# Turning one batch's x on TensorE instead of by transposing transfers, in a fused attention and highway layer

## The chip, the core and the metric

The kernel runs on one core of one Trainium2 chip. The time is that of one execution in device microseconds (us), from the first to the last thing the core does; lower is better. A profile is one execution recorded instruction by instruction. Engines are called as the profile calls them: PE is the matmul engine (PEld its weight loads, which overlap), DVE the vector engine, ACT the scalar engine, POOL the general one, SP the one that here only issues transfers. "DVEq" or "SPq" is an engine's queue of issued work. SBUF is the on-chip memory that transfers and all engines reach, PSUM the small memory that PE writes its products to, in banks.

## What is computed

Attention with cosine scores over 8 batches of 12 heads, 448 tokens of 64 numbers each, then a gated layer over the 3584 tokens with all 12 heads side by side (768 numbers a token). Cut to what matters:

```python
q_n = q / (norm(q) + 1e-6);  k_n = k / (norm(k) + 1e-6)
attn = softmax(q_n @ k_n.T / tau) @ v            # (8, 12, 448, 64)
x = attn.transpose(0, 2, 1, 3).reshape(3584, 768)
H = maximum(x @ w_h, 0)
T = 1 / (1 + exp(-(x @ w_t + b_t)))
out = T * H + (1 - T) * x                        # float32
```

The kernel works in 16-bit floats between the two ends.

## The kernel before

**Work units.** A batch has six head pairs; they are numbered through, pair s = 6 * batch + p, from 0 to 47. Tokens of a batch are three blocks of 128 and a tail of 64. For a pair, q and k rows are scaled to length one (`scaled`, ops named qn and kn; on POOL or DVE), turned so that the 64 head numbers lie across partitions (`turn`: for batches 0 to 3 seven transposes on PE and a copy cpT out of PSUM; for batches 4 to 7, the tuple `BY_DMA`, one transposing transfer for two pairs on SP's queue, line 570, and one for the tails, line 597), multiplied (`scores`: three ops qk and one qkt on PE, each followed by an exponential on ACT, lines 646 and 662), and multiplied with v (`attend`: three ops av and a tail avt on PE; then a reciprocal rc, line 720, and the scaled output ev, line 722, on DVE, which writes the pair's columns of the tile x). Squares, their sums in halving steps (fa, fb, fc) and the inverse root (nt, or ln and re on ACT for batches 0 to 2) come a batch ahead (`square`, `newton`).

**The gated layer.** When the six pairs of a batch have written x, `ffn` (line 742 on) runs it in four groups, i = 0 to 3: three of 128 tokens and the tail of 64; groups are numbered g = 4 * batch + i. A group needs its x turned, with the 768 numbers across partitions; the turned x lies in the tile xT, a half of a batch in each of its two buffers. There are two ways to turn it. For batches 1 to 6, SP issues two transposing transfers a batch (`xd12` for groups 0 and 1, `xd9` for groups 2 and 3, line 759). For batches 0 and 7, each group has an op xt6 (xt3 for the tail) on PE, that turns six (three) blocks of 128 x 128 against a unit matrix into a pB bank of PSUM (line 765), and a copy cpx6 (cpx3) on DVE from there to xT (line 770). Then PE multiplies with both weights (ops fft3 and fft4 of lines 843 and 850, ffc of the tail at 834), ACT makes the tanh of the gate (874), DVE forms hm (888), gt (893) and gg (896), POOL or DVE adds x (out, 901), and a transfer stores it (910).

**Modes of PE.** Every PE op carries a mode letter: F for products over all 128 partitions (turns, qkt, av, xt), T for two halves of 64 partitions side by side (qk, fft), C for two halves of the output (ffc).

**Buffers.** PSUM has three double banks pS, for scores qk and the products of the gated layer, and two banks pB, for turned blocks, the qkt products and the outputs U of a pair. An op that takes a bank waits until the last reader of its former content is done.

**What sets the order.** The function first makes a list of 1683 ops, each with an engine and what it reads, writes and uses. A written-out permutation, ORDER, says in which order they are issued; each engine works through its own ops in that order, and semaphores carry the waits between engines. SLOTS gives the buffer for each new use of a tile, one digit each, in the same order. MOVED is a set of op numbers: where an op may run on either of two engines, `pick` takes the other one for the numbers in it. URGENT is a set of POOL ops for which the next DVE op of those that share a port with POOL waits. Op numbers count the ops in the order in which the function makes them, so they shift behind an added op.

Of the kernel before, what the change touches and what calls it, by code (L numbers as in the profile page):

```python
# [102 lines left out]
URGENT = frozenset(  # L103
    int(n)
    for n in """
116 117 135 136 154 155 174 192 307 327 345 365 383 403 434 448 502 510 529 548 586 604 636 716 735 754 811 857
916 923 958 976 992 1010 1054 1079 1113 1120 1137 1155 1173 1208 1237 1251 1276 1316 1317 1334 1351 1369 1370
1404 1434 1448 1473 1548 1584
""".split()
# [912 lines left out]
```

## Time and profile before

| what | value |
|---|---|
| three timed runs | 267.65, 266.72, 264.89 us; median 266.72 |
| the profiled execution's own time | 266.79 us |
| its span (first to last instruction) | 265.0 us |
| PE busy | 241.9 us, 91% of the span |
| DVE, ACT, POOL busy | 219.5, 205.5, 120.2 us |
| mean granted clock of PE | 0.995 of full |
| transposing transfers on SP | 12 into xT, 12 into qT, 4 into tT |
| 128 x 128 transposes of x on PE | 42 |

How to read the rows below. A row of the timeline has start, length, engine, line, operation, tiles out and in, shape and count, and in brackets the idle time of the engine before it with what ended that idle. A row of the groups has line, engine, operation, tiles, shapes and count, then busy time in us and the mean of one in ns, then idle before. A row of the stretches has the stretch and its length, then for each engine its busy time and its number of instructions, then PE's granted clock, the mean busy share of the 16 DMA engines (it can pass 1 because packets of several queues overlap) and GB/s. A row of the waits has who waited for whom, total us, number and longest. A length on PE is a pipelined one: the next instruction can start before it ends, so what an op costs PE is read from start to start.

### The profile page before, as it was taken

What the parts mean: (1) busy time and instruction counts of PE and PEld (TensorE: products, weight loads), DVE (VectorE), ACT (ScalarE), POOL (GpSimd) and SP (SyncE); (2) the same over time, 40 slices, a digit from 0 to 9 for tenths busy, and PEclk for the clock granted to TensorE, in tenths of its full rate; (3) what the DMA queues carried; (4) which work ended last, traced back from release to release, by engine and by line L of the source; (5) the groups of instructions that cost most, each with busy time, mean ns of one, the idle gap of its engine ahead of it and who ended that gap; (6) DMA issues with size and microseconds to landing.
All of it is one profiled execution on the core that took longest, in us unless ns stands there. A gap on an engine that the chain in (4) does not pass through costs nothing. (4 is left out here: it accounts for less than half of the span.)

```text
span 265.0 us, 9021 instructions
## 1 busy us (share of the span) xinstructions
PE 241.9 (91%) x3747; PEld 163.4 (62%) x3747; DVE 219.5 (83%) x478; ACT 205.5 (78%) x334; POOL 120.2 (45%) x154
## 2 busy tenths in 40 slices
PE   0787889999999999999999799999999999999990
PEld 0344567667676676667665566567667677667560
DVE  4799999989799999999999969988867774457484
ACT  2279999899988999899989798689877997572130
POOL 8873676384752546714633507244455300123220
PEclk9999999999999999999999999999999999999998
DMA  6999999999999799999899989996665988300244
GB/s 132 199 192 180 178 205 204 194 185 186 165 190 208 116 188 165 175 170 230 174 136 131 153 201 239 154 223 168 144 116 141 218 113 177 118 2 25 112 143 158
DMA packets 103353, 43.12 MB, mean 163 GB/s; under 512 B 97168, under 2 KB 100240, under 8 KB 103312
## 3 DMA queue, kind: packets, MB, share of 16 engines
q0 software_dynamic: 38464, 16.32, 51.3%
q1 hardware_dynamic: 62560, 23.63, 47.8%
q10 hardware_dynamic: 2288, 2.59, 3.4%
q8 instruction: 29, 0.48, 0.7%
q14 instruction: 12, 0.10, 0.1%
HBM read 37.82 MB, written 11.01 MB: 184 GB/s over the span
## 5 line engine op out<-in xcount | busy, mean ns | idle before, releaser
L646 ACT ACTIVATE E<-pS 128x896 f16<-128x896 f32 x144 | 127.7, 931 | 21.5 <-PE pS L640 19.0
L850 PEld LDWEIGHTS <-xT 64*128 64x128 f16 x1152 | 53.5, 94 | 33.8 <-DMA xT<-x 1.7
L850 PE MATMUL pS<-wt,xT 64*128 64x384 f16 x576 | 57.7, 323 | 1.2 <-DMA xT<-x 1.2
L850 PE MATMUL pS<-wh,xT 64*128 64x384 f16 x576 | 56.9, 323 | 0.2 <-DVE hm L888 0.2
L901 POOL TENSOR_TENSOR os<-x,hm 128x768 f32<-128x768 f16 (+1 forms) x15 | 20.9, 1398 | 61.4 <-DVE hm L896 33.7
L640 PE MATMUL pS<-qT 64*128 64x384 f16 x288 | 44.1, 326 | 1.9 <-ACT E L646 1.2
L696 PE MATMUL pB<-vp,E 128*128 128x65 f16 x864 | 44.2, 194 | 0.4 <-ACT E L646 0.4
L696 PEld LDWEIGHTS <-E 128*128 128x128 f16 x864 | 38.7, 98 | 3.0 <-issue 1.0
L888 DVE SCALAR_TENSOR_TENSOR hm<-pS,x 128x768 f16<-128x768 f32 (+1 forms) x32 | 26.8, 839 | 13.4 <-PE pS L850 11.0
L640 PEld LDWEIGHTS <-qT 64*128 64x128 f16 x576 | 23.3, 94 | 17.7 <-issue 4.5
L692 PE MATMUL pB<-vp,Et 128*128 128x130 f16 x144 | 31.9, 222 | 0.8 <-DVE x L722 0.8
L874 ACT ACTIVATE tt<-pS 128x768 f16<-128x768 f32 x24 | 19.5, 821 | 14.9 <-PE pS L850 14.6
L722 DVE SCALAR_TENSOR_TENSOR x<-pB,rd 128x448 f16<-128x448 f32 x48 | 29.6, 619 | 1.1
L662 ACT ACTIVATE Et<-pB 128x64 f16<-128x64 f32 x96 | 29.2, 370 | 1.0 <-PE pB L655 0.8
L640 PE MATMUL pS<-tT,qT 64*128 64x64 f16 x282 | 27.5, 189 | 0.0
L255 POOL TENSOR_TENSOR qn<-kr,rs 128x384 f16<-128x384 f16 x20 | 17.6, 882 | 14.4 <-DVE qn L255 5.4
L720 DVE RECIPROCAL rd<-pB 128x7 f32<-128x7 f32 x48 | 9.6, 199 | 12.8 <-PE pB L696 6.5
L712 PE MATMUL pB<-vp,E 128*128 128x65 f16 x288 | 18.4, 194 | 0.0
L255 POOL TENSOR_TENSOR qn<-qr,rs 128x384 f16<-128x384 f16 x18 | 15.0, 840 | 6.4 <-DVE qn L255 2.8
L307 PE MATMUL pB<-fill 128*128 128x384 f16 x40 | 9.8, 404 | 8.4 <-DVE fill L278 8.4
L896 DVE TENSOR_TENSOR hm<-tt,hm 128x768 f16<-128x768 f16 (+1 forms) x31 | 17.2, 558 | 0.2
L255 POOL TENSOR_TENSOR kb<-kt,rs 64x384 f16<-64x384 f32 x10 | 8.2, 821 | 20.2 <-DVE tt L893 6.9
(117 smaller groups left out, 439.3 us busy)
## 6 DMA issues: line engine op xcount, KB each, us to landing
out_dram<-os SPq DMA_DIRECT2D x20, 384.0 KB, 3.5
vr<-in_v_dram POOLq DMA_DIRECT2D x8, 576.0 KB, 8.6
kr<-in_k_dram POOLq DMA_DIRECT2D x7, 576.0 KB, 14.3
qr<-in_q_dram POOLq DMA_DIRECT2D x7, 576.0 KB, 12.3
qt<-in_q_dram SPq DMA_DIRECT2D x16, 96.0 KB, 6.7
vt<-in_v_dram SPq DMA_DIRECT2D x16, 96.0 KB, 6.7
out_dram<-os ACTq DMA_DIRECT2D x4, 384.0 KB, 3.0
kt<-in_k_dram SPq DMA_DIRECT2D x14, 96.0 KB, 6.4
```

Source lines behind the costliest of these rows:

```text
L255: return (nc.vector if eng == "DVE" else nc.gpsimd).tensor_mul(out_, a, c)
L640: ins = nc.tensor.matmul(dst, lhsT=qT[ln, 384 + 128 * c : 512 + 128 * c], rhs=rhs, start=True, stop=True)
L646: return nc.scalar.activation(R("E", s)[:, c, :, 0:448], R("S", 3 * s + c)[:, :, 0:448], AF.Exp, scale=inv_tau)
L662: ins = nc.scalar.activation(R("Et", s)[:, at : at + n], R("B", ("S", s))[:, lo : lo + n], AF.Exp, scale=inv_tau)
L692: nc.tensor.matmul(U[:, 2 * c : 2 * c + 2, :].rearrange("p g e -> p (g e)"), lhsT=Et[:, 192 + 128 * c : 320 + 128 * c], rhs=vp[:, 6:8, :]. ...
L696: ins = nc.tensor.matmul(U[:, 2 * c + ab, :], lhsT=EF[:, j, 576 * ab + 128 * c : 576 * ab + 128 * c + 128], rhs=vp[:, 3 * ab + j, :], star ...
L712: ins = nc.tensor.matmul(U[:, 6, :], lhsT=lt, rhs=rh, start=(n == 0), stop=(n == 7))
L722: op("DVE", f"ev {s}", lambda: nc.vector.scalar_tensor_tensor(out=R("x", b)[:, :, D * p : D * p + D], in0=U_()[:, :, 0:D], scalar=0.0, in1 ...
L850: ins = nc.tensor.matmul(P[:, h, 0:MH], lhsT=lt, rhs=rh, start=(part == 0 and cc == (-1 if wi == 0 else 0)), stop=(part == 1 and cc == CC ...
L874: return nc.scalar.activation(T.rearrange("p (h m) -> p h m", h=2), P[:, :, 0:MH], AF.Tanh, scale=0.5)
L888: return nc.vector.scalar_tensor_tensor(out=o_, in0=i0, scalar=0.0, in1=xs, op0=ALU.max, op1=ALU.subtract)
L901: op(en, f"out{wd} {g}", lambda: eng.tensor_add(R("os", g)[:, 0:W], xall(), R("hm", g)[:, 0:W]), at + 0.1, r=[("gg", g), ("x", b)], w=[("o ...
```

## The change

x of batch 3, the fourth, is turned the second way: the new tuple `X_ON_PE = (3,)` sends it to the branch of batches 0 and 7. Its two transposing transfers (xd12 and xd9, groups 12 to 15) go; four ops on PE come (xt6 for groups 12, 13, 14 and xt3 for group 15) and four copies on DVE (cpx6, cpx6, cpx6, cpx3). The list has 1689 ops instead of 1683.

ORDER, SLOTS, MOVED and URGENT are all new, so the order on every engine, the buffer of most uses, and the engine of many ops that may run on either are different. The numbers of buffers are the same as before. Counted over the two lists: PE has 669 ops instead of 665, DVE 473 instead of 467, ACT 294 instead of 300, POOL 148 instead of 145, SP 105 instead of 106. By kind, DVE gets four copies of xT, three copies cpT (from ACT), six of v (from ACT and POOL), two of v's tails, one tail output add and three clears; it loses four folds fa and fb of 12 columns and one of 36, three kn, one qn, two norms of query tails and two squares. ACT loses three copies cpT and four of v and gets two squares.

The diff, with the four tables cut to their ends:

```diff
 ORDER = tuple(
     int(n)
     for n in """
-25 23 4 0 20 19 33 5 18 17 21 29 22 16 27 6 24 35 10 26 1 277 28 36 41 11 8 42 7 3 12 73 15 31 87 30 80 43 44 32
...
-1663 1673 1671 1664 1672 1674 1665 1676 1666 1675 1677 1679 1678 1680 1681 1682
+25 23 5 0 20 19 33 16 18 17 21 26 22 7 9 28 4 24 36 10 27 1 12 481 29 35 41 686 32 42 2 3 11 84 6 31 8 80 30 82
...
+1687 1688
...
 URGENT = frozenset(
...
-1404 1434 1448 1473 1548 1584
...
+1357 1358 1375 1411 1454 1520 1572 1607 1638 1671
...
 MOVED = frozenset(
...
-1512 1513 1532 1548 1549 1551 1566 1568 1583 1584 1586 1601 1603 1632 1665
...
+1573 1574 1589 1590 1607 1638 1671
...
     BY_DMA = (4, 5, 6, 7)
     LOGS = 2
+    X_ON_PE = (3,)
     assert (B, NH, S, D) == (8, 12, 448, 64)
...
-        if 1 <= b < B - 1:
+        if 1 <= b < B - 1 and b not in X_ON_PE:
             if not i % 2:
                 hf = i // 2
                 nd = 12 - 3 * hf
```

On PE's new list the four turns stand thus, with their neighbours: fft3 10 1 1, **xt6 12**, qkt 24, fft3 10 0 2; then fft3 12 0 3, **xt6 13**, **xt6 14**, fft3 12 1 3; then qk 26 0, **xt3 15**, av 24 0. (In these names the first number of fft3 is the group, that of qk, qkt and av the head pair.)

More of the change, by code (lines that the diff above doesn't have):

```diff
@@ L91 @@
     for n in """
-0000010100000001000000100011002011000200001101111011001120011211010200021101000210000101210001121100001200010110
-1212120110011101101000010211001002021010102111101212101020011002001020102001021001001001211001021212020010011210
-0001100101001011010200102200010200010102102102212011020000000100212211211000211021120111101000011120011122010002
-0012101102103001020001102011021011002001110021110110221000001020101100200002103101100100021110020011222012100021
-0121011010021210011110112302001121112100002101012010221111201120011010002101220122100012221100220101201100020100
-2011000110310221021211000020010021001001001210020100010220112101111002210320101021121201100201112211101000000210
-0003212210120112000102122111010222201021010110011100100020100012110012201200002111020101320210002122211020022021
-00031201100010110120100020102011212022011001110
+0000011010000100010002001001101001100010000112100010012110121020201000010012010102120001010100120101110001020112
+0011200011110000010200010111022000101102111002101100100200210101210200111002100101012100101121012200211000010000
+2201011102100100200122101001001122001021002022010220122010001102000201120110021010211112011001111021120011010100
+2012003102000102120120110201101200211101112101000100210001010102100120010200230110111200110102100101020022112202
+2101111012010101011101010200203110011001021002102100010120221001100110102110100010121120212110200212101111121000
+1000210111100012011002220022102121110322011002120021010000000020021101212002101120012000011231102010011110203201
+1002001100120121020002211012101100020001021010020012202120110103200111020022200100102012001111121220311111221011
+000012001010201010002111110020120021012020021120301
 """.replace("\n", "")
@@ L105 @@
     for n in """
-116 117 135 136 154 155 174 192 307 327 345 365 383 403 434 448 502 510 529 548 586 604 636 716 735 754 811 857
-916 923 958 976 992 1010 1054 1079 1113 1120 1137 1155 1173 1208 1237 1251 1276 1316 1317 1334 1351 1369 1370
-1404 1434 1448 1473 1548 1584
[3 rows of a table added]
 """.split()
```

143 rows, old and new, of tables (MOVED, ORDER, URGENT) are left out of this document.

## The prediction

> **What bounds the kernel now.** I read the page's engine totals first, then the same totals by stretches, then who PE waited for in the stretch that the change touches, and last the single rows there.
>
> ```profile
> span 265.0 us, 9021 instructions
> PE 241.9 (91%) x3747; PEld 163.4 (62%) x3747; DVE 219.5 (83%) x478; ACT 205.5 (78%) x334; POOL 120.2 (45%) x154
> ```
>
> ```profile
> core 0: us, PE busy (x) PEld busy (x) DVE busy (x) ACT busy (x) POOL busy (x), PEclk, DMA share, GB/s
> 8.00:60.00 52.00, 46.86 (x646) 30.50 (x646) 48.82 (x107) 44.70 (x78) 33.94 (x48) 1.00 1.42 192
> 60.00:110.00 50.00, 49.30 (x812) 34.53 (x811) 47.39 (x102) 45.19 (x73) 27.94 (x34) 1.00 1.26 174
> 110.00:130.00 20.00, 19.97 (x323) 13.42 (x321) 18.80 (x46) 19.22 (x29) 7.44 (x10) 1.00 1.07 192
> 130.00:150.00 20.00, 17.99 (x261) 11.88 (x258) 19.73 (x39) 16.35 (x29) 10.65 (x12) 1.00 1.54 138
> 150.00:170.00 20.00, 19.06 (x336) 12.93 (x332) 16.57 (x37) 17.75 (x30) 6.73 (x7) 1.00 1.12 200
> 170.00:250.00 80.00, 80.00 (x1275) 54.81 (x1273) 54.48 (x117) 58.03 (x94) 23.70 (x28) 1.00 0.63 134
> ```
>
> PE sets the time: from 170 to 250 it has no idle at all, so whatever delays PE before 170 arrives whole at the end, and whatever frees PE before 170 is gained whole. Its idle time lies in two places: 52.00 - 46.86 = 5.1 us in 8 to 60 (the start, where PE, DVE and ACT are all between 86 and 94% busy) and 2.0 + 0.9 = 2.9 us in 130 to 170. In the first of these two late stretches DVE is the busiest engine (19.73 of 20 us) and the share of the DMA engines is the highest of all stretches, 1.54. That is where the fourth batch's x is turned and used.
>
> Who PE waited for from 120 to 175:
>
> ```profile
> PE pS L850 <- DMA xT<-x: 1.2, 2, 1.0
> PE pB L692 <- DVE x L722: 0.8, 1, 0.8
> PE pB L655 <- DVE x L722: 0.6, 1, 0.6
> PE pS L850 <- DVE hm L888: 0.3, 1, 0.3
> ```
>
> These four make 2.9 us: all of PE's idle there. The two transfers of the change stand in the SP queue, and in PE's row stands what came of the second one; the last line is the time from issue to landing of the two:
>
> ```profile
> 127.96 2.07 SPq L759 DMA_TRANSPOSE xT<-x  x1
> 134.94 3.92 SPq L759 DMA_TRANSPOSE xT<-x  x1
> ```
>
> ```profile
> 148.87 0.34 PE L850 MATMUL pS<-wt,xT 64*128 64x384 f16 x2 [0.98 <-DMA xT<-x]
> ```
>
> ```profile
> DMA to landing us min/median/max: 4.3/9.1/13.9
> ```
>
> The second transfer was issued at 134.94 and landed 13.9 us later, at 148.8; PE stood still for 0.98 us and went on at 148.87. The rest of the 1.2 us is a wait on the fifth batch's first transfer:
>
> ```profile
> 168.28 0.34 PE L850 MATMUL pS<-wt,xT 64*128 64x384 f16 x2 [0.23 <-DMA xT<-x]
> ```
>
> **The change part by part.** *Turning on PE.* Four ops are added: three of six 128x128 transposes (xt6) and one of three (xt3), 21 in all. Their price, and that of a change of PE's mode, from places where the kernel already does it:
>
> ```profile
> 57.21 0.51 PE L765 MATMUL pB<-ident,x 128*128 128x128 f16 x6
> 57.55 0.50 PE L580 MATMUL pB<-ident,qn 128*128 128x128 f16 x6
> ```
>
> ```profile
> 61.18 0.33 PE L640 MATMUL pS<-qT 64*128 64x384 f16 x2
> ...
> 61.37 0.33 PE L640 MATMUL pS<-qT 64*128 64x384 f16 x2
> ...
> 61.66 0.23 PE L692 MATMUL pB<-vp,Et 128*128 128x130 f16 x1
> ```
>
> Six transposes keep PE for 57.55 - 57.21 = 0.34 us (the printed 0.51 is a pipelined span), so 21 cost 3.5 x 0.34 = 1.2 us. They run beside nothing: PE does one thing at a time. *The new order's mode changes.* A score step followed by another of its mode takes 61.37 - 61.18 = 0.19 us, and followed by an op of another mode 61.66 - 61.37 = 0.29: a change costs 0.10. Walking both ORDER lists over PE's ops by their mode letter gives 136 changes before and 143 after, so 7 x 0.10 = 0.7 us (4 of the 7 stand before the tail product of head pair 18, 3 between that and pair 32's, none later). Together PE has 1.9 us more to do, none of it in the last third.
>
> *The two transfers that go.* They take 2.07 + 3.92 us of SP's queue and a share of the DMA engines where that is scarcest. SP only issues, and the wait that it caused is the 1.0 us on PE above; freed SP time I price at nothing, because what stands behind in the queue waits for DVE's or POOL's results. Freed DMA room could shorten the wait of 0.23 us at 168.28 and this one, of DVE on a store that had not landed, with the wait of PE that follows it:
>
> ```profile
> 155.38 0.96 DVE L901 TENSOR_TENSOR os<-x,hm 128x768 f32<-128x768 f16 x1 [2.47 <-DMA out_dram<-os]
> ```
>
> ```profile
> 160.92 0.19 PE L655 MATMUL pB<-tT 128*128 128x64 f16 x1 [0.62 <-DVE x L722]
> ```
>
> PE's 0.62 us for DVE's x comes 5.5 us after DVE's stop, and I count it with the DMA waits. The removal is worth between 1.0 us (the one wait) and 2.9 us (all four).
>
> *The copies that come.* Each xt needs a copy out of PSUM on DVE, and takes one of the two pB banks until that copy is done. Also MOVED changes who does what: counted by `pick` over the two lists, DVE goes from 467 to 473 ops, ACT from 300 to 294, POOL from 145 to 148. ACT is below 90% around the change except in 110 to 130, so its relief I price at nothing; POOL is at half or less. DVE is what matters. Between its outputs for head pairs 18 and 28 (counted from 0; the first is the row below, the other comes right behind the store's row above, at 157) DVE's list changes, kinds that cancel and one small step (rs from n) left out, by: minus one k norm, two q norms, one key-tail norm, one query-tail norm, one full output add; plus two tail output adds, one copy of qT, four copies of xT, one sum, one square, one gate, one fold. Rows:
>
> ```profile
> 109.45 0.62 DVE L722 SCALAR_TENSOR_TENSOR x<-pB,rd 128x448 f16<-128x448 f32 x1
> ```
>
> ```profile
> L255 DVE TENSOR_TENSOR qn<-qr,rs 128x384 f16<-128x384 f16 x29 | 16.5, 577 | 0.1
> L255 DVE TENSOR_TENSOR qn<-kr,rs 128x384 f16<-128x384 f16 x27 | 15.9, 594 | 0.1
> L901 DVE TENSOR_TENSOR os<-x,hm 128x768 f32<-128x768 f16 x14 | 13.9, 991 | 2.7 <-DMA out_dram<-os 2.7
> L418 DVE TENSOR_TENSOR f<-sq 128x1152 f16<-128x1152 f16 x16 | 13.1, 816 | 0.0
> L424 DVE TENSOR_REDUCE n<-f 128x36 f32<-128x576 f16 x16 | 11.8, 740 | 0.0
> L893 DVE TENSOR_SCALAR tt<-tt 128x768 f16<-128x768 f16 x24 | 10.2, 425 | 2.3 <-POOL os L901 1.7 <-ACT tt L874 0.6
> L258 DVE COPY qT<-pB 128x896 f16<-128x896 f16 x16 | 9.8, 615 | 2.8 <-PE pB L583 2.8
> L255 DVE TENSOR_TENSOR sq<-kr 128x1152 f16<-128x1152 f16 x9 | 7.0, 788 | 0.0
> L255 DVE TENSOR_TENSOR kb<-qt,rs 128x384 f16<-128x384 f32 x6 | 3.4, 569 | 0.0
> L255 DVE TENSOR_TENSOR kb<-kt,rs 64x384 f16<-64x384 f32 x6 | 3.3, 552 | 0.1
> L770 DVE COPY xT<-pB 128x768 f16<-128x768 f16 x6 | 3.2, 550 | 0.1
> L901 DVE TENSOR_TENSOR os<-x,hm 128x384 f32<-128x384 f16 x2 | 1.1, 550 | 0.0
> L770 DVE COPY xT<-pB 128x384 f16<-128x384 f16 x2 | 0.7, 350 | 0.0
> ```
>
> Minus 0.594 + 2 x 0.577 + 0.552 + 0.569 + 0.991 = 3.9; plus 2 x 0.550 + 0.615 + 3 x 0.550 + 0.350 + 0.740 + 0.788 + 0.425 + 0.816 = 6.5: DVE has 2.6 us more there, 2.0 of it the copies of xT. DVE's idle from 110 to 170 is 60 - 55.1 = 4.9 us, 2.47 of it behind the store. So the 2.6 us just fit if the store's wait goes; the cover is thin. Their cost on PE is bounded by 0 below (a longer DVE list gives PE nothing) and by 2.6 above.
>
> *The new order elsewhere.* ORDER and the buffer choices change everywhere. In 60 to 110 PE has 0.7 us of idle and in 170 to 250 none, so no order can gain there, and it can lose. In 8 to 60 there is 5.1 us to gain. DVE's and ACT's lists do nearly the same work there (one square goes from DVE to ACT ahead of the first scores, the clearing of the two kb buffers from POOL to DVE), so I take nothing, between -2.5 (half of that idle) and +1 (a fifth of it more).
>
> **The sum**, against the profiled execution's own time, 266.79 us (span 265.0 and 1.8 around it), which is 0.07 above the median of the runs, 266.72: 266.8 + 1.2 (transposes) + 0.7 (mode changes) - 2.9 (the waits between 130 and 170) + 0 = 265.8. I take the upper end of the gain because the transfer's wait goes for certain, the store and the transfer behind share the DMA room that comes free, and the remaining two waits, 1.1 us, hang on where DVE's list puts the two x outputs, which the new list moves anyhow.
>
> **The rivals.**
> *DVE becomes the bound (slower).* In 110 to 150 DVE is busy 38.5 of 40 us. If its list is what paces 109 to 157, the 2.6 us come on top of the stretch, PE's 1.5 us there (transposes and three mode changes) vanish in its waits, and the four mode changes ahead of it stay: 266.8 + 2.6 + 0.4 = 269.8. For it: three of the four waits above, 1.7 us, are on DVE, two of them for a pB bank, and four more users come to those two banks. Against it: DVE's 4.9 us of idle. It decides once less than 2.6 us of that idle can be filled.
> *The transfer was hidden but for its own wait (no change).* Only the 1.0 us goes; the DVE waits have their own cause and stay, and so does the 0.23: 266.8 + 1.9 - 1.0 = 267.7.
> *The start gains too (faster).* The new orders close some 2.5 of the 5.1 us in 8 to 60: 265.8 - 2.5 = 263.3. For it: those waits are short ones among engines that all have slack. Against it: the lists there carry the same work.
> *Each transpose costs its full latency.* If a transpose kept PE from start to end, the 0.22 us that a single one shows at 57.89 would give 21 x 0.22 = 4.6 us instead of 1.2, and 269.2.
>
> ```profile
> 57.89 0.22 PE L583 MATMUL pB<-ident,kb 128*128 128x128 f16 x1
> ```
>
> The Trainium skill, page "VectorE: DVE Perf Modes", section "The three transpose paths", gives 390 ns for a 128x128 transpose on TensorE and 1309 ns for the transfer; 21 x 390 ns would be an estimate of 8.2 us on the engine that bounds, and about 273 us by this sum. The rows say otherwise: six follow each other in 0.34 us.
>
> **How the numbers follow.** Waits closed, 265.8: 0.38 (its own range 264.3 to 267.2). No change, 267.7: 0.16. Start gains, 263.3: 0.24. DVE bound, 269.8: 0.20. Full latency: 0.02. About 1% (2.7 us) is what a measurement can tell from no change here, so faster means under 264.05 and slower over 269.4. Faster: the start's 0.24 and the edge of the first, 0.27. Slower: most of DVE's 0.20 and half of the last, 0.18. The same: 0.55. The range from 262.9 to 269.8 cuts off the lower part of the start's case and half of DVE's, under 0.2 together.
>
> **What would show it.** Right: no PE wait on xT near 148, line 765 with 63 matmuls instead of 42, 26 DMA transposes instead of 28, DVE near 20 of 20 us through 130 to 150, PE's idle from 130 to 170 under 1 us. Wrong: PE waiting for DVE's xT copies or for pB behind them, PE idle moved ahead of 60 in either direction, or a stretch 170 to 250 that is no longer full.

## The result and the profile after

The changed kernel takes **263.9 us** (median of 14 runs, 263.2 to 265.0), the kernel before 266.8 us on the same chip (14 runs, 264.6 to 270.9): ratio 0.991, 95% interval 0.988 to 0.994. Run once more on another chip it took 263.6 us, ratio 0.985 (0.980 to 0.990). So it is faster by about 1 to 1.5%; forecast were 265.8 us in 262.9 to 269.8, with "the same" as the likeliest word. The ratios leave disturbed runs of either kernel out and so need not be the quotient of two medians: 0.991 is a gain of 2.5 us, where the medians differ by 2.9. The profiled execution of after took 263.22 us (span 261.4), the shortest of its 14, and that of before lay at the median of its own; so the 3.6 us between the two profiles, which are taken apart below, are up to 1.1 us more than the gain.

Totals of after, from its page:

```profile
span 261.4 us, 9058 instructions
...
PE 241.5 (92%) x3768; PEld 163.5 (63%) x3768; DVE 217.0 (83%) x487; ACT 203.9 (78%) x329; POOL 124.1 (47%) x154
```

PE is busy as long as before (241.9 us) in a span that is 3.6 us shorter. By stretches of after:

```profile
core 0: us, PE busy (x) PEld busy (x) DVE busy (x) ACT busy (x) POOL busy (x), PEclk, DMA share, GB/s
8.00:60.00 52.00, 45.88 (x646) 29.71 (x644) 47.87 (x105) 45.49 (x78) 33.14 (x44) 1.00 1.42 192
60.00:110.00 50.00, 49.59 (x825) 35.81 (x823) 47.09 (x103) 48.22 (x78) 27.58 (x33) 1.00 1.27 177
110.00:130.00 20.00, 20.00 (x321) 13.36 (x320) 19.43 (x41) 17.01 (x28) 10.53 (x13) 1.00 1.06 197
130.00:150.00 20.00, 20.00 (x296) 12.72 (x293) 19.89 (x45) 16.18 (x26) 9.72 (x11) 1.00 1.24 175
150.00:170.00 20.00, 20.00 (x350) 13.77 (x347) 19.55 (x46) 18.30 (x32) 8.26 (x10) 1.00 0.83 147
170.00:250.00 80.00, 80.00 (x1273) 54.35 (x1273) 51.09 (x114) 55.59 (x89) 25.97 (x29) 1.00 0.60 131
```

From 130 to 170 PE's idle has gone from 2.9 us to none, and DVE stands at 19.89 and 19.55 of 20 us. The list of who PE waited for from 60 to 250 has one row left; the transfer into xT and the two rows for DVE's x are gone:

```profile
PE pS L852 <- DVE hm L890: 0.3, 1, 0.3
```

(Lines of the changed kernel are two higher from the branch on.) The groups show the new work, with the transposes 63 instead of 42 and nine long copies instead of six:

```profile
L767 PE MATMUL pB<-ident,x 128*128 128x128 f16 x63 | 5.2, 221 | 0.0
L772 DVE COPY xT<-pB 128x768 f16<-128x768 f16 x9 | 4.8, 551 | 0.8 <-PE pB L767 0.7
```

and the timeline has xt6 13 and xt6 14 between two steps of the gated layer: twelve transposes from 136.98 to 137.76, no bracket on any of them:

```profile
136.98 0.84 PE L767 MATMUL pB<-ident,x 128*128 128x128 f16 x12
137.76 0.66 PE L852 MATMUL pS<-wh,xT 64*128 64x384 f16 x6
```

**Where the 3.6 us came from.** I went through PE's list op by op in both traces, from each op's start to the next one's, and set each step against the usual step of its kind (the median of that kind where nothing holds it up) with the 0.10 us for a change of mode. The first turn of batch 0's x on PE starts at 42.27 before and 42.20 after: the start gives nothing (-0.07). From there to PE's end the usual steps add up to 1.60 us more (the transposes and six of the seven mode changes), and the time beyond the usual steps falls by 4.60 us, 3.8 of them between 130 and 175 (4.61 to 0.82). PE's last product group starts 3.08 us earlier, and what follows it to the end of the span is 0.5 us shorter. Before, then after:

```profile
257.52 1.16 PE L811 MATMUL pB<-wh,xT 128*64 128x192 f16 x24
```

```profile
254.44 1.16 PE L813 MATMUL pB<-wh,xT 128*64 128x192 f16 x24
```

-0.07 + 1.60 - 4.60 - 0.5 = -3.6.

### The profile page after: what moved, and what is told of

The parts are those of the page before. It is cut to its first block, busy times and chain, and to the rows that moved or that the text cites. A ratio compares the mean times of both kernels' runs of the same rounds, so it can differ in the third digit from the quotient of the medians.

```text
span 261.4 us, 9058 instructions
## 1 busy us (share of the span) xinstructions
PE 241.5 (92%) x3768; PEld 163.5 (63%) x3768; DVE 217.0 (83%) x487; ACT 203.9 (78%) x329; POOL 124.1 (47%) x154
## 4 chain that ended last, share of the span: by engine, by line
PE 81%; DVE 13%; DMA 2%; issue 1%; ACT 1%; SPq 1%; DVEq 0%; ACTq 0%
PE pS L852 38%; PE pS L642 10%; PE pB L698 9%; PE pS L836 5%; PE pB L714 4%; PE pB L657 4%; PE pB L694 3%; PE pB L582 3%; DVE qn L257 2%; PE pB L309 2%; PE pB L767 2%; DVE sq L257 2%; DMA first<-in_q_dram 2%; DVE x L724 2%; DVE f L420 1%
## 5 line engine op out<-in xcount | busy, mean ns | idle before, releaser
L852 PE MATMUL pS<-wt,xT 64*128 64x384 f16 x576 | 56.3, 323 | 0.0
L642 PE MATMUL pS<-qT 64*128 64x384 f16 x288 | 43.3, 327 | 2.1 <-ACT qT L260 1.0
L903 POOL TENSOR_TENSOR os<-x,hm 128x768 f32<-128x768 f16 (+1 forms) x14 | 20.0, 1430 | 38.4 <-DVE hm L898 21.1
L642 PEld LDWEIGHTS <-qT 64*128 64x128 f16 x576 | 22.4, 94 | 18.1 <-issue 3.7
L257 POOL TENSOR_TENSOR qn<-kr,rs 128x384 f16<-128x384 f16 x23 | 19.1, 830 | 22.7 <-DVE qn L257 7.0
L257 POOL TENSOR_TENSOR qn<-qr,rs 128x384 f16<-128x384 f16 x19 | 16.2, 864 | 4.9 <-DVE hm L898 2.2
L694 PEld LDWEIGHTS <-Et 128*128 128x128 f16 x144 | 14.0, 97 | 5.4 <-issue 3.1
L898 DVE TENSOR_TENSOR hm<-tt,hm 128x768 f16<-128x768 f16 (+1 forms) x31 | 16.5, 543 | 0.3
```

The costliest lines, as they stand in the source:

```text
L257: return (nc.vector if eng == "DVE" else nc.gpsimd).tensor_mul(out_, a, c)
L642: ins = nc.tensor.matmul(dst, lhsT=qT[ln, 384 + 128 * c : 512 + 128 * c], rhs=rhs, start=True, stop=True)
L694: nc.tensor.matmul(U[:, 2 * c : 2 * c + 2, :].rearrange("p g e -> p (g e)"), lhsT=Et[:, 192 + 128 * c : 320 + 128 * c], rhs=vp[:, 6:8, :]. ...
L852: ins = nc.tensor.matmul(P[:, h, 0:MH], lhsT=lt, rhs=rh, start=(part == 0 and cc == (-1 if wi == 0 else 0)), stop=(part == 1 and cc == CC ...
L903: op(en, f"out{wd} {g}", lambda: eng.tensor_add(R("os", g)[:, 0:W], xall(), R("hm", g)[:, 0:W]), at + 0.1, r=[("gg", g), ("x", b)], w=[("o ...
```

## The experiments

Three theories went into the first four kernels. A: PE's waits between 130 and 170 go because the turn moved from transfers to PE, in any order. B: the new order alone does it. C: what counts is the room that the two transfers leave. The four ran on one chip, where the kernel before took 268.4 us (265.9 to 270.8).

**The swap alone.** The kernel before with its own order; x of batch 3 turned on PE, the four turns and copies put in where their inputs are ready (qkt 24 moved beside one of them).

```diff
+    X_ON_PE = (3,)
...
-        if 1 <= b < B - 1:
+        if 1 <= b < B - 1 and b not in X_ON_PE:
```

> The kernel before with its own order, buffers and engines; only x of batch 3 is turned on PE (two transfers out, four PE ops and four DVE copies in, one qkt op moved behind them to free its bank). PE has 21 transposes (1.2 us) and two mode changes (0.2) more, DVE 2.0 us of copies, with nothing taken off it. Theory A (what is gained is PE's waits between 130 and 170, and turning on PE removes them in any order): 266.8 + 1.4 - 3 = 265.2 us, PE idle from 130 to 170 under 1 us. Rival B (the gain comes from the new order; in the old one the copies push DVE's list): 266.8 to 268.8 us, with DVE waits in place of the transfer's.

Measured: 266.25 us, ratio 0.994 (0.991 to 0.997). The waits of its PE after 60, longest first:

```profile
PE pB L657 <- DVE xT L772: 0.8, 1, 0.8
PE pS L642 <- DVE qT L260: 0.5, 1, 0.5
PE pS L852 <- DVE hm L890: 0.5, 2, 0.4
PE pB L694 <- DVE x L724: 0.4, 1, 0.4
PE pS L852 <- DMA xT<-x: 0.2, 1, 0.2
```

The transfer's 1.0 us has gone and only the fifth batch's 0.2 is left. A new wait has come: a copy of xT stands behind an hm in DVE's list and holds a pB bank for 0.8 us. The swap alone is worth about 1.5 us, between theory A (265.2) and rival B (266.8 at least): the transfer's wait goes in the old order too, but the old DVE list gives part of the gain back.

**The new order alone.** The changed kernel with `X_ON_PE` empty: its order, but the two transfers again, issued as soon as x is there.

```diff
-    X_ON_PE = (3,)
+    X_ON_PE = ()
```

> The kernel after with its new order, buffers and engines, but x of batch 3 turned by the two transposing transfers again, the first right behind the last x output, the second right behind the last product that reads its buffer. PE has 1.2 us of transposes and two mode changes (0.2) less. Theory A: the waits for the transfer and for DMA room come back, some 3 us: 263.9 - 1.4 + 3 = 265.5. Rival B (the order alone makes the gain): 263.9 - 1.4 = 262.5 us, with no PE wait on xT.

Measured: 269.38 us, ratio 1.007 (1.003 to 1.010). Theory B (262.5) falls: the order needs the turn on PE. Theory A (265.5) is 3.9 us short as well, because the wait that comes back is far longer than in the old order and the clock falls with it (last section). SP's rows and the row of PE that waits for them:

```profile
131.93 5.38 SPq L760 DMA_TRANSPOSE xT<-x  x2
...
138.09 6.04 SPq L571 DMA_TRANSPOSE qT<-qn  x1
```

```profile
138.40 1.14 PE L851 MATMUL pS<-wt,xT 64*128 64x384 f16 x6 [3.91 <-DMA xT<-x]
```

The new order wants xT at 138.40 - 3.91 = 134.5, 2.6 us after the transfers are issued, and gets it after 6.5. On PE and DVE the turn takes 1.6 us: in the changed kernel xt6 13 starts at 136.98, and PE reads what it turned at 138.61. Swap and order are worth -1.5 and +1.8 us alone, and about -2.5 to -4 together: neither part can be priced without the other.

**The transfers as ghosts.** The changed kernel, with the two transposing transfers issued beside it into spare memory that nothing reads.

```diff
+            if b in X_ON_PE and not i % 2:
+                hf = i // 2
+                nd = 12 - 3 * hf
+                op("SP", f"gd{nd} {b} {hf}", lambda: nc.sync.dma_start(
+                    spare[hf], R("x", b)[:, 4 * hf : 4 + 3 * hf, :].rearrange("l h m -> l (h m)"),
+                    transpose=True), key, r=[("x", b)], w=[("spare", hf)])
```

> The kernel after, and the two transposing transfers of batch 3 issued all the same, into places that nobody reads, at the positions of the new order where their data are ready. PE and DVE do what they do in the kernel after; DMA engines and SP's queue carry what they carried before. Rival C (part of the gain is DMA room that came free: DVE's 2.5 us stop on a store, PE's 0.62 and 0.23): 263.9 + 0.9 to 2.5 = 264.8 to 266.4 us. If only the wait on the transfer itself mattered: 263.9 us, the same.

Measured: 268.09 us (265.4 to 271.8), ratio 0.998 (0.994 to 1.002): about 4 us over the changed kernel's 263.9 and 263.6 (on other chips), though nobody reads the ghosts. SP's rows, then the two new waits of PE:

```profile
131.14 2.13 SPq L770 DMA_TRANSPOSE first<-x  x1
133.32 3.98 SPq L770 DMA_TRANSPOSE spare<-x  x1
...
138.13 6.13 SPq L574 DMA_TRANSPOSE qT<-qn  x1
```

```profile
149.11 0.34 PE L644 MATMUL pS<-qT 64*128 64x384 f16 x2 [1.76 <-DMA qT<-qn]
...
179.57 0.34 PE L644 MATMUL pS<-qT 64*128 64x384 f16 x2 [1.49 <-DVE hm L899]
```

The first wait is the ghosts' doing. The transfer into qT behind them is issued at 138.13 and lands 10.9 us later, at 149.0; PE could have gone on at 149.11 - 1.76 = 147.35. In the changed kernel it is issued at 132.18, lands 7.9 us later, at 140.1, and PE reads it at 146.74:

```profile
132.18 2.93 SPq L572 DMA_TRANSPOSE qT<-qn  x1
```

```profile
146.74 0.34 PE L642 MATMUL pS<-qT 64*128 64x384 f16 x2
```

So the changed kernel has 146.74 - 140.1 = 6.6 us of slack there; the ghosts take 8.9, in an execution that runs some 0.5 us later at that point. The second wait follows a copy of v on DVE that stood 2.1 us for a load issued at 165.83; the copy came 12.1 us after that issue, 10.5 after it in the changed kernel. That is a load that came late, and I can't put it down to the ghosts. Shown as their cost is thus the first wait, 1.8 us of the 4; theory C's range, 264.8 to 266.4, holds 263.9 + 1.8 = 265.7, though not the measured time.

**No turn at all.** The kernel before without the two transfers; x of the fourth batch is not turned, so that its gated layer works on what an older batch left in xT.

```diff
-        if 1 <= b < B - 1:
+        if b == 3:
+            pl.slot["xT", (b, i // 2)] = 1 - i // 2
+        elif 1 <= b < B - 1:
```

> The kernel before with its own order, and the two transfers left out with nothing in their place: x of batch 3 is not turned, groups 12 to 15 multiply what lay in xT. This is the most that taking the transfers out can give in the old order, at no cost. Theory A with the DMA room counted (all four waits, 2.9 us and the refilling behind them): 263 to 263.9 us. Only the transfer's own wait: 266.8 - 1.0 to 1.2 = 265.7 us, with the DVE waits at 146 and 161 still there.

Measured: 264.76 us, ratio 0.988 (0.984 to 0.993). Waits of PE after 60:

```profile
PE pB L692 <- DVE x L722: 0.8, 1, 0.8
PE pS L640 <- DVE qT L258: 0.5, 1, 0.5
PE pS L852 <- DVE hm L890: 0.4, 2, 0.3
```

Without any turning, the old order keeps the 0.8 us for DVE's x and loses both waits on xT and the 0.6, which I had counted with the DMA waits. The time lies between the two forecasts (263 to 263.9, and 265.7): part of the DVE waits hung on the transfers, part did not. So even a free turn would give that order only about what the changed kernel has.

**Plain ghosts, from ACT's queue and from SP's.** To part the bytes from the transposing, the same bytes were moved as plain copies in rows of 256 bytes, read by nothing: once issued by ACT, once by SP where the transposing ghosts had stood. They ran on two further chips (kernel before 267.2 on both). The diff is against the transposing ghosts; the version for SP has `"SP"` and `nc.sync` in it.

```diff
-                op("SP", f"gd{nd} {b} {hf}", lambda: nc.sync.dma_start(
-                    spare[hf], R("x", b)[:, 4 * hf : 4 + 3 * hf, :].rearrange("l h m -> l (h m)"),
-                    transpose=True), key, r=[("x", b)], w=[("spare", hf)])
+                op("ACT", f"gd{nd} {b} {hf}", lambda: nc.scalar.dma_start(
+                    spare[hf], R("x", b)[:, 4 * hf : 4 + 3 * hf, :].rearrange("l h m -> l (h m)").rearrange(
+                        "l (j c) -> l j c", c=128)), key, r=[("x", b)], w=[("spare", hf)])
```

> The changed kernel with as many bytes as the two removed transfers carried, moved SBUF to SBUF as plain copies in rows of 256 bytes, issued from ACT's queue at the places where the removed transfers stood; nothing reads them, the output is the same. With the removed transposing transfers put back as ghosts on SP's queue the time was 268.1, ratio 0.998. Theory C1 (what those cost was DMA engine time, whoever issues): the plain copies cost a good part of that too, 265 to 267, and the transfers and stores that follow them land later than in the changed kernel. Theory C2 (what those cost was SP's queue, blocked while it issues a transposing transfer, so that the qT transfers behind are issued late): within 0.5 us of the changed kernel, 263.9, the qT transfers issued at the changed kernel's times, and ACT at most 0.3 us busier.

> As the kernel with the plain ghost copies (the bytes of the two removed transfers, rows of 256 bytes, read by nothing), but issued from SP's queue at the places of the removed transfers, where the transposing ghosts stood. Theory C1 (the DMA engines' time is what counts): as with ACT's queue, 2 to 3 us over the changed kernel or about as much as the transposing ghosts, and the transfers behind land late. Theory C2 (SP's queue, busy while it issues a transposing transfer): issuing a plain one takes SP under 2 us, the qT transfers are issued when they are in the changed kernel, and the time is within 1 us of the changed kernel.

Measured: from ACT 266.85 us (264.8 to 270.3), ratio 1.002 (0.998 to 1.006); from SP 263.93 us (263.5 to 265.2), ratio 0.987 (0.982 to 0.991), beside 263.64 of the changed kernel on the same chip. From SP the bytes cost nothing. SP's rows:

```profile
130.85 0.67 SPq L770 DMA_DIRECT2D spare<-x  x1
131.58 1.76 SPq L770 DMA_DIRECT2D first<-x  x1
133.43 3.44 SPq L368 DMA_DIRECT2D vt<-in_v_dram  x1
136.97 3.19 SPq L574 DMA_TRANSPOSE qT<-qn  x1
```

and the time from issue to landing of that qT transfer, in the changed kernel, with transposing and with plain ghosts:

```profile
DMA to landing us min/median/max: 7.9/7.9/7.9
```

```profile
DMA to landing us min/median/max: 10.9/10.9/10.9
```

```profile
DMA to landing us min/median/max: 8.3/8.3/8.3
```

The plain ghosts do delay it, to 136.97 + 8.3 = 145.3, but that is still within the slack; the transposing ones make it 3.7 us later still, and pass it. The kernel with the plain copies on ACT's queue shows what SP's queue has to do with it. There SP issues the transfer at 132.41, nearly as early as in the changed kernel, and it lands 12.9 us later, again at 145.3:

```profile
132.41 4.51 SPq L574 DMA_TRANSPOSE qT<-qn  x1
```

So the plain bytes delay it by 5.2 us whichever queue issues them: where it lands follows theory C1 (the DMA engines' time, whoever issues) and not C2 (SP held up). The time of the version for SP is nevertheless the one that C2 gave, within 1 us, and not C1's 2 to 3 us more, because a delay costs nothing up to the slack of 6.6 us, which neither theory had counted. Transposing ghosts from another queue were not run, so whether their further 3.7 us are DMA time or SP's later issue (138.13 instead of 136.97) stays open. The Trainium skill, page "Advanced Engine Details and Errata", section "DMA Advanced Topics", says that transposing transfers on this chip are as fast as regular ones. These runs don't decide that: the two transposing ghosts landed 7.3 and 11.8 us after their issue, the plain ones 6.5 and 8.9 us from SP and 9.0 and 13.9 us from ACT, each in a crowd of its own.

For the time of the kernel the copies from ACT were a poor instrument. ACT works through its list in order, so its next exponential stood behind the issue of the ghost, which has to wait for x: it starts 1.2 us after ACT was free, where the changed kernel has no gap.

```profile
130.85 0.69 ACTq L770 DMA_DIRECT2D spare<-x  x1
131.58 0.92 ACT L650 ACTIVATE E<-pS 128x896 f16<-128x896 f32 x1 [1.17 <-PE pB L659]
```

PE's list shows a new wait of 1.0 us on ACT's tt soon after. That reading is argued from the rows, and they are those of an execution of 264.8 us; what put the median 2 us above it is not shown. For the time, the run from SP is the one that counts.

**The price of a transpose.** Every one of the 21 new transposes issued twice, and in another kernel four times, into the same place.

```diff
-                for j in range(nb):
+                for j in list(range(nb)) * (4 if b in X_ON_PE else 1):
```

> The changed kernel with each of the 21 transposes of the fourth batch's x issued twice into the same place; the output is the same. If a transpose is paid at the pipelined step of 0.056 us (six in 0.34 us) on an engine that is the bound: 263.9 + 1.2 = 265.1, and the line of the transposes shows 84 of them. If it is paid at the 0.22 us of a single one: 263.9 + 4.6 = 268.5. If PE has room there (rival: something else paces the stretch): 263.9. The Trainium skill, page 'VectorE: DVE Perf Modes', section 'The three transpose paths', gives 390 ns for one; an estimate by that is 8.2 us more.

> The changed kernel with each of the 21 transposes of the fourth batch's x issued four times into the same place (63 more); the output is the same. Pipelined step as I priced it, six in 0.34 us, on a PE that is the bound: 63 x 0.056 = 3.6 us over the changed kernel, about 267.5. At the 0.22 us of a single one: 63 x 0.22 = 13.9 us, 278. If PE has room (rival): the same time as the changed kernel.

Measured: twice 265.59 us, ratio 0.999 (0.995 to 1.003); four times 267.47 us, ratio 1.002 (0.999 to 1.004), on the chip where the changed kernel took 263.64. That is 3.83 us for 63 transposes, 0.061 each: PE is the bound there, and the pipelined step of 0.34 us for six (0.057) is the price, not the 0.22 of a single one. The group's busy time says the same, (8.7 - 5.2) / 63 = 0.056:

```profile
L767 PE MATMUL pB<-ident,x 128*128 128x128 f16 x126 | 8.7, 220 | 0.0
```

The doubled ones came out 1.9 us over 263.64, but across chips, where 1.2 was expected. In their trace the 24 transposes of xt6 13 and xt6 14 take 139.61 - 138.16 = 1.45 us from start to start, where 12 took 137.76 - 136.98 = 0.78: 0.056 for each added one.

**DVE's cover.** The four new copies done twice on DVE; and, in another kernel, done once on ACT.

```diff
+            def copy_x():
+                for _ in range(2 if b in X_ON_PE else 1):
+                    ins = nc.vector.tensor_copy(xTg().rearrange("p c l -> p (c l)"), R16(("T", ti))[:, 0 : 128 * nb])
+                return ins
```

```diff
+            def copy_x():
+                to, of = xTg().rearrange("p c l -> p (c l)"), R16(("T", ti))[:, 0 : 128 * nb]
+                return nc.scalar.copy(to, of) if b in X_ON_PE else nc.vector.tensor_copy(to, of)
```

> The changed kernel with each of the fourth batch's four copies of xT out of PSUM done twice: the row xT<-pB 128x768 took 0.55 us and 128x384 0.35 us, so DVE gets about 2.0 us more between 130 and 160, and the output is the same. Theory A (TensorE is the bound there and DVE has cover): the time stays within 0.5 us of the changed kernel, 263.9, and PE's idle from 130 to 170 stays under 1 us. Rival D (DVE's list is what paces 109 to 157, as my prediction's rival says; the 2.6 us that the change brings just fit): the copies come on top, up to 265.9, and PE shows waits on DVE x, DVE xT or hm of 1 to 2 us there.

> The changed kernel with the fourth batch's four copies of xT out of PSUM on ACT instead of DVE; the output is the same. With these copies done twice on DVE, PE waited 1.2 + 0.8 us for DVE near 140 and 1.4 us at 179.6. If DVE's list is only just below being the bound there (as the doubled copies say): taking 2.0 us off it gains nothing, because PE already has no wait there; the time stays within 0.5 us of the changed kernel, DVE's busy time from 130 to 160 falls by about 2 us, and ACT, 16.2 of 20 us from 130 to 150, takes them. If ACT cannot take them (rival): PE waits for ACT's E or xT appear between 138 and 155 and the time rises by 1 us or more.

Measured: twice on DVE 266.53 us, ratio 1.002 (0.998 to 1.005); on ACT 265.22 us, ratio 0.996 (0.992 to 1.001), 1.6 over the changed kernel on its chip. PE's waits with the doubled copies:

```profile
140.05 1.15 PE L856 MATMUL pS<-wt,xT 64*128 64x384 f16 x12 [0.83 <-DVE xT L774]
141.97 0.34 PE L642 MATMUL pS<-qT 64*128 64x384 f16 x2 [0.77 <-DVE hm L894]
...
179.59 0.34 PE L642 MATMUL pS<-qT 64*128 64x384 f16 x2 [1.23 <-DVE hm L894]
```

PE lost 1.9 us near 140 (start to start) for 2.0 us of added copies: DVE's list has no room left there. The wait at 179.59 follows a copy of v that stood 1.9 us for a load, as with the ghosts, and is not the copies' doing for sure. That is rival D; its bound of 265.9 was passed by 0.6 us, less than this second wait. On ACT the copies are no better, as the rival there said: 0.6 us of waiting for tt at 135 and three shorter waits up to 144, 1.5 us in all, start to start. The prediction's words for DVE, "the cover is thin", were right: the changed kernel uses all of it.

**Fewer mode changes.** Five score products (the expectation says six) moved beside ops of their own mode, 143 changes down to 134; nothing else. The moves in ORDER, by name:

```
qk 8 1  -> before turn 9          qk 33 2 -> before ffc3 15 1 0
qkt 8   -> before turn 10         qk 43 0 -> before qk 42 1
(exponential of qkt 8 with it)    qk 42 2 -> before qkt 44
```

> The changed kernel with six score products moved by a few places so that they stand beside PE ops of their own mode (two in head pair 8 near the start, the rest near 200 to 250): mode changes on PE 143 to 134, nothing else changed. If a change costs the 0.10 us that I read from two neighbouring steps, and PE is full: 9 x 0.10 = 0.9 us less, 263.0, and the step of PE from 170 on shows it. If the 0.10 is no cost of the change but of that op (rival): 263.9 within 0.3. If the moved score products starve ACT's exponentials or a PSUM bank: above 263.9, with a new PE wait on ACT.

Measured: 266.39 us, ratio 1.001 (0.998 to 1.005), slower than the changed kernel. Moved products came before their PSUM bank was free:

```profile
164.90 0.34 PE L642 MATMUL pS<-qT 64*128 64x384 f16 x2 [0.82 <-ACT E L648]
...
215.63 0.34 PE L642 MATMUL pS<-qT 64*128 64x384 f16 x2 [0.63 <-ACT E L648]
```

From batch 0's turn to PE's end it takes 2.5 us more: 3.3 to 3.6 us of new stalls near 50 to 65, at 165 and near 215, and 0.8 to 1.0 us less in all other steps (by how they are sorted into kinds), where nine changes at 0.10 us were to give 0.9. The price fits, the idea fails: moved ahead, the products come before ACT has read their banks.

**The changed kernel again**, as a control on the chip of the last three kernels.

> The changed kernel itself, unaltered, once more, so that the three kernels beside it and the last four have a time of it to stand against. The comparison after the prediction gave 263.9 us, ratio 0.991. If that ratio holds: 0.987 to 0.995, and no PE wait over 0.6 us behind the first 20 us. If it was partly luck of those runs (rival): a ratio of 0.995 or more, and kernels such as the one with doubled transposes (265.6 on their chip) come out no worse than this one.

Measured: 263.64 us (six runs, 263.4 to 268.4), ratio 0.985 (0.980 to 0.990). The gain is no luck of the first runs. No version tried beats the changed kernel.

## Why the prediction was right, and where its sum was not

The mechanism held: PE sets the time, its waits from 130 to 170 go, and the turn and the mode changes cost about what the rows said. The range held too, but it is 7 us wide and lies on both sides of no change; the sum itself was 1.9 us high. It forecast a gain of 1.0 us, and 2.5 to 2.9 came on this chip. Between the two profiles the gap is 3.6 - 1.0 = 2.6 us: 0.9 for waits that were priced too low, 0.8 for stalls elsewhere, 0.5 at the end, 0.3 for a cheaper turn and mode changes, 0.1 at the start.

- *The turn on PE, +1.2 us.* Right, by the fourfold transposes: 21 x 0.061 = 1.3.
- *The mode changes, +0.7 us.* Near in price, by the moved score products. Together with the turn, from batch 0's turn on, they measure 1.60 us where 1.2 and six changes at 0.10 make 1.8.
- *The waits that go, -2.9 us.* Right in place and mis-sized: they measure -3.8. The bracket of a wait begins where the modelled end of the matmul before it lies, but the next one could have started 0.17 us earlier, since PE's instructions overlap. In the kernel before, the step from the two bth products to the next product took 148.87 - 147.56 = 1.31 us round the bracket of 0.98:

```profile
147.56 0.33 PE L850 MATMUL pS<-bth,ones 64*128 64x384 f16 x2
```

In the changed kernel the same step, unhindered, takes 138.61 - 138.45 = 0.16:

```profile
138.45 0.33 PE L852 MATMUL pS<-bth,ones 64*128 64x384 f16 x2
138.61 0.49 PE L852 MATMUL pS<-wt,xT 64*128 64x384 f16 x4
```

So that stall cost 1.15 us, not 0.98, and the four others of the sum likewise cost 0.43, 0.93, 0.78 and 0.40 us where their brackets say 0.27, 0.77, 0.62 and 0.23. The five make 3.7 of the 3.8 measured.
- *"In 60 to 110 PE has 0.7 us of idle ..., so no order can gain there".* Wrong by 0.8 us over the rest of the list: for example a stall of 0.70 us for DVE's qT at 106.94 is gone, and one of 0.43 for hm at 103.21 came in its place. What is left, 0.5 us, is the shorter end after the start of PE's last matmul, 6.6 us before and 6.1 after; the two other kernels in the old order have 6.4 and 6.2, so some of it varies from run to run. Neither was in the sum.
- *"Freed SP time I price at nothing".* Not refuted for SP: with the plain copies on ACT's queue, which leave SP free, the qT transfer lands as late as with those on SP's. What the price left out is the delay of the transfers behind: the qT transfer has slack of 6.6 us in the changed kernel, and the two transposing transfers put back use it up and make PE wait 1.76 us.
- *"The store and the transfer behind share the DMA room".* Half borne out: the plain bytes delay the transfer behind by 5.2 us, but the slack takes that up and the time stays. DVE's wait on stores in 60 to 270 went from 2.7 us to 0.6 without the turn in the old order, and in the new order it is 0.4 us or none with ghosts, but 0.7 in the control and 1.6 in the fourfold kernel, which have none; so the transfers are not what decides it there, and what does stays open.
- *Rival "DVE becomes the bound", 269.8.* It did not happen, but 2 us more on DVE make it so.
- *Rival "hidden but for its own wait", 267.7.* Refuted: the DVE waits went too, part by the removal (no turn, old order: one of the two stays), part by the new list.
- *Rival "the start gains too", 263.3.* Nearest in time and wrong in cause: PE reaches batch 0's turn 0.07 us earlier.
- *Rival "each transpose costs its full latency", 269.2.* Refuted by the fourfold transposes.
- The signs of being right came as said: no wait on xT, 63 transposes, 26 transposing transfers, DVE 19.89 of 20, no PE idle from 130 to 170. One sign of being wrong came as well: PE's idle in 8 to 60 went from 5.1 to 52.00 - 45.88 = 6.1 us. It cost no time: PE ran 646 instructions in that stretch in both, and reached batch 0's turn 0.07 us earlier.

## What to carry to other kernels

Price a stall of a pipelined engine from start to start, not by its bracket; the difference, 0.17 us here, comes once per stall. A transposing transfer can cost more than the wait on its own result: look how much slack the transfers behind it on the queue have. When a step moves to other engines, the order must move with it, and the two can't be priced apart: here -1.5 and +1.8 us alone made -2.5 to -4 together.

## What the runs showed of the hardware that I had not expected

In the kernel with the new order alone, PE's granted clock fell to half during the stop of 3.91 us and stayed there for about 5 us of work behind it. Stretches of that kernel:

```profile
134.00:138.00 4.00, 0.49 (x6) 0.10 (x2) 3.71 (x10) 1.32 (x3) 1.29 (x2) 0.84 1.42 194
138.00:140.00 2.00, 1.60 (x12) 0.78 (x14) 0.61 (x3) 0.00 (x0) 1.17 (x1) 0.50 1.67 198
...
142.00:144.00 2.00, 2.00 (x20) 1.03 (x18) 0.00 (x0) 0.23 (x1) 0.70 (x1) 0.61 1.39 171
144.00:146.00 2.00, 1.53 (x22) 0.89 (x18) 0.77 (x1) 2.00 (x4) 0.00 (x0) 1.00 1.33 233
```

The third last number of a row is the clock: 0.84, 0.50 up to 142, 0.61, then 1.00. If it is either full or half, a mean of 0.84 over the first row puts the fall at 136.7, 2.2 us after the stop began at 134.5, and 0.61 puts the return at 143.6. PE worked at half speed from 138.4 to then, 5.2 us, which is an estimate of 2.6 us on top of the 3.9. The Trainium skill, page "TensorE: Matmul & The Clock Gate", section "Part 1: The HAM clock gate", has half clock after an idle window of about 3.4 us. This trace agrees that a stop of 3.91 us halves the clock, but the fall came before 3.4 us of it had passed.
